# Loading q for two chunks at a time in an attention + MLP kernel, with later stores, halved stripes and two moved chunks

## The chip, the cores and the metric

The kernel runs on one core of one Trainium2 chip. The metric is device time of one execution in microseconds (us); the kernel before takes 227 us. A run is called slow when it lies over 1.5% above the fastest of its kernel. Ratios use fast runs; the medians quoted are of all runs of a kernel, slow ones included.

Engines are named as in the profile: PE is the matrix engine, PEld its weight load, DVE the vector engine, ACT the scalar engine, POOL GpSimd, SP the engine that only issues DMAs here ("SPq" is its queue). A DMA is cut into packets that run on up to 16 DMA engines.

## The reference, cut to what matters

```python
# q, k, v: [4 batches, 8 heads, 768 tokens, 64];  lam: one decay per head
# linear attention with decay, in blocks of tokens, with a running state per head
for b in range(nb):
    intra = (q_b @ k_b.T * Dmask) @ v_b
    inter = (q_b * lam_pow) @ kv_state
    out[b] = intra + inter
    kv_state = lam_block * kv_state + (k_b * rev_pow).T @ v_b
x = out, tokens by (head, dim)           # [3072, 512]
h = x @ w_in                             # [3072, 2048]
g = where(h >= 1, h, where(h <= -1, 0, (h + 1)**2 / 4))
return g @ w_out                         # [3072, 512] float32
```

## The kernel before

There are 24 chunks of 128 tokens (six to a batch) and six stripes of four chunks. For each chunk q, k and v are loaded, q and k are scaled and cast to bf16 on POOL (k of the first four on DVE), transposed (on PE for the first six chunks, by DMA after that), and PE makes the attention output `po`, which ACT casts into `xT`. For each stripe PE makes `h` (512 tokens by 16 blocks of 128), ACT and DVE the activation, and PE the output rows, which ACT copies to an output buffer `osb` and SP stores. The MLP of a stripe is interleaved with the attention of the next ones.

All instructions are emitted in an order that a small planner in the kernel computes beforehand; every engine then works through its own queue in order. SP's queue holds loads, DMA transposes and stores together. An SP entry whose data are not ready holds up everything behind it.

```python
def f_load(c, x, wait):                       # one chunk, one of q, k, v: 256-byte runs
    t = ld.tile([128, H, D], F32, ...)
    nc.sync.dma_start(out=t, in_=(q, k, v)[x][b, :, s0:s0 + C, :].rearrange("h p d -> p h d"))
def f_qx(c):                                  # transpose by DMA, chunks 6 to 23
    nc.sync.dma_start_transpose(out=qT[c], in_=qs[c].rearrange("p h d -> p (h d)"))
def f_x(c):
    nc.scalar.copy(out=xT[sx][:, :, off:off + C], in_=pot[c])
def f_st(s, ms):                              # store: 128 rows of 2 KB
    nc.sync.dma_start(out=out[m0:m0 + 128, :], in_=osb[s, ms])
...
QS = (1, 2)          # stripes whose first matmul is done chunk by chunk (128 columns)
op = tile_pool(bufs=3)                        # output buffers
add(("st", y), "SP", 550, ..., due=-1, dma=780)   # a store goes before any load
# (cut: everything else)
```

## Time and profile before

| What | Value | From |
|---|---|---|
| time, median of 4 runs | 227.14 us | runs |
| span, granted clock | 225.5 us, 0.996 | profile |
| PE busy | 205.6 us | engine table |
| first matmul | 7.5 us | timeline |
| 256-byte, 2 KB packet, median | 18 ns, 85 ns | DMA packet records |
| store, issue to landing | 2.6 us | DMA issues |

These are the lines of the page for the kernel before: busy tenths of PE in 40 slices of the span (5.6 us each), granted clock in tenths, and busy share of the DMA engines.

```profile
PE   0497989999999989689999999999999999999992
PEclk9999999999999999999999999999999999999998
DMA  6999999999898797999999999999011001110212
```

PE is full except for the fill (the first four slices), a dip around slices 14 to 17 (79 to 101 us), and the tail. DMA is busy until 157 us.

The waits of PE in the kernel before, from 60 us on (who waited for whom, total us, times, longest):

```profile
PE pu L266 <- ACT vi L235: 2.3, 2, 1.7
PE ph L332 <- ACT xT L312: 1.0, 1, 1.0
PE py L365 <- issue: 0.2, 1, 0.2
```

So about 3.3 us of PE time are lost after 60 us. Before that there is the fill, and PE's first matmul waits 7.5 us for the first k. `vi` is the cast of v, which waits for v's load. The SP queue before, in that stretch (start us, us, what):

```profile
80.93 0.58 SPq L406 DMA_DIRECT2D x2f<-in_v_dram  x1
82.03 0.36 SPq L374 DMA_DIRECT2D out_dram<-osb  x1
82.45 2.07 SPq L406 DMA_DIRECT2D x1f<-in_k_dram  x1
84.63 1.21 SPq L256 DMA_TRANSPOSE kT<-ks  x1
85.95 1.19 SPq L260 DMA_TRANSPOSE qT<-qs  x1
87.19 0.57 SPq L406 DMA_DIRECT2D x0f<-in_q_dram  x1
87.82 0.57 SPq L406 DMA_DIRECT2D x2f<-in_v_dram  x1
```

SP has hardly a pause: as soon as one entry is issued the next is (the longest pause here is 0.5 us, before the store). Loads, transposes and stores take turns.

### The profile page before, as it was taken

The page shows a single profiled execution, that of the slowest core. Times are in us where ns is not written, and L with a number is a line of the kernel's source. Part 1 is how long each engine was busy: PE and PEld are TensorE (multiplying, and loading weights), DVE is VectorE, ACT ScalarE, POOL GpSimd, SP SyncE. Part 2 cuts the span into 40 slices and gives each one's busy share as a digit, 9 for nine tenths or more (in the row PEclk, how much of TensorE's full clock was granted, in tenths as well). Part 3 has the DMA queues.
Part 4 walks back from the last instruction along what each step waited for, and adds up shares of the span by engine and source line. Part 5 has one row for each costly group of instructions (what it writes and reads, how often), then busy time and mean ns, then how long its engine had stood idle before and what let it go on. Part 6 is the DMA issues. An engine that isn't in the chain of part 4 may idle for free.

```text
span 225.5 us, 4385 instructions
## 1 busy us (share of the span) xinstructions
PE 205.6 (91%) x1733; PEld 123.4 (55%) x1760; DVE 144.2 (64%) x218; ACT 123.6 (55%) x220; POOL 61.0 (27%) x65
## 2 busy tenths in 40 slices
PE   0497989999999989689999999999999999999992
PEld 0376634765888577567664554545545544444441
DVE  7687399978498948567655956856656564554300
ACT  3346867544678285546757575676655444455121
POOL 6543560056034332423342542361000000000000
PEclk9999999999999999999999999999999999999998
DMA  6999999999898797999999999999011001110212
GB/s 121 216 218 170 195 189 202 200 223 196 212 202 158 182 215 169 205 173 204 225 196 237 214 166 233 232 211 211 0 49 47 24 22 49 47 47 16 77 67 77
DMA packets 102837, 34.38 MB, mean 152 GB/s; under 512 B 95136, under 2 KB 99744, under 8 KB 102816
## 3 DMA queue, kind: packets, MB, share of 16 engines
q1 hardware_dynamic: 97920, 29.90, 70.4%
q0 software_dynamic: 4752, 4.19, 12.2%
q8 instruction: 14, 0.23, 0.5%
q14 instruction: 7, 0.06, 0.1%
q10 hardware_dynamic: 144, 0.00, 0.0%
HBM read 27.27 MB, written 6.29 MB: 149 GB/s over the span
## 4 chain that ended last, share of the span: by engine, by line
PE 57%; SPq 3%; DMA 2%; issue 1%; ACT 1%; ACTq 0%
PE py L365 27%; PE ph L332 23%; PE po L305 3%; DMA x2f<-in_v_dram 2%; PE ps L285 2%; SPq L406 1%; PE po L302 1%; PE pu L266 1%; SPq L256 1%; SPq L260 1%; ACT vi L235 0%; ACT osb L370 0%; PE pt L285 0%; ACTq L370 0%
## 5 line engine op out<-in xcount | busy, mean ns | idle before, releaser
L332 PE MATMUL ph<-xT,w_in_sb 128*128 128x128 bf16 (+1 forms) x741 | 92.5, 268 | 1.9 <-ACT xT L312 1.0
L365 PE MATMUL py<-w_out_sb,gT 128*128 128x512 bf16 x368 | 92.6, 379 | 1.0 <-issue 0.2
L340 ACT ACTIVATE r<-ph,one 128x512 bf16<-128x512 f32 (+2 forms) x96 | 64.6, 678 | 47.7 <-PE ph L332 38.4
L332 PEld LDWEIGHTS <-w_in_sb 128*128 128x128 bf16 x752 | 52.5, 98 | 29.0 <-issue 2.2
L365 PEld LDWEIGHTS <-gT 128*128 128x128 bf16 x384 | 35.7, 98 | 38.8 <-DVE gT L356 0.2
L348 DVE TENSOR_SCALAR t<-r 128x1024 bf16<-128x1024 bf16 x48 | 25.2, 526 | 42.7 <-ACT r L340 42.7
L356 DVE TENSOR_TENSOR gT<-w,t 128x1024 bf16<-128x1024 bf16 x48 | 39.8, 828 | 1.6
L231 POOL TENSOR_TENSOR ks<-x1f,tab_k 128x512 bf16<-128x512 f32 x20 | 22.1, 1103 | 62.0 <-DMA x1f<-in_k_dram 48.9
L351 DVE TENSOR_TENSOR w<-r,t 128x1024 bf16<-128x1024 bf16 x48 | 37.2, 775 | 1.5
L231 POOL TENSOR_TENSOR qs<-x0f,tab_q 128x512 bf16<-128x512 f32 x24 | 28.5, 1189 | 25.7 <-DMA x0f<-in_q_dram 25.3
L235 ACT CAST vi<-x2f 128x512 bf16<-128x512 f32 x24 | 14.8, 616 | 16.5 <-DMA x2f<-in_v_dram 16.4
L295 DVE TENSOR_TENSOR sc<-ps,causal 128x512 bf16<-128x512 f32 x20 | 13.8, 689 | 13.6 <-PE pt L285 13.6
L370 ACT COPY osb<-py 128x512 f32<-128x512 f32 x24 | 14.1, 586 | 15.1 <-PE py L365 13.4
L305 PE MATMUL po<-sc,vi 128*128 128x128 bf16 x192 | 19.2, 226 | 0.2
L312 ACT CAST xT<-po 128x512 bf16<-128x512 f32 x24 | 14.0, 585 | 7.2 <-PE po L305 6.6
L270 ACT CAST ubd<-pu 64x256 bf16<-64x256 f32 x40 | 14.6, 364 | 5.3 <-PE pu L266 5.0
L305 PEld LDWEIGHTS <-vi 128*128 128x128 bf16 x192 | 15.2, 102 | 2.3 <-issue 0.6
L302 PE MATMUL po<-qT,ubd 128*128 128x128 bf16 x80 | 15.1, 224 | 0.0
L295 DVE TENSOR_TENSOR sc<-pt,causal 128x512 bf16<-128x512 f32 x20 | 13.6, 680 | 0.0
L266 PE MATMUL pu<-vi,ks 128*128 128x128 bf16 x80 | 8.4, 232 | 2.4 <-ACT vi L235 2.3
L241 PE MATMUL pt<-ident,ks 128*128 128x128 bf16 x24 | 3.1, 266 | 8.0 <-DVE ks L231 7.8
L266 PEld LDWEIGHTS <-ks 128*128 128x128 bf16 x80 | 6.4, 105 | 5.5 <-issue 3.1
(48 smaller groups left out, 87.4 us busy)
## 6 DMA issues: line engine op xcount, KB each, us to landing
x1f<-in_k_dram SPq DMA_DIRECT2D x24, 256.0 KB, 4.8
x0f<-in_q_dram SPq DMA_DIRECT2D x24, 256.0 KB, 4.4
x2f<-in_v_dram SPq DMA_DIRECT2D x24, 256.0 KB, 4.6
out_dram<-osb SPq DMA_DIRECT2D x24, 256.0 KB, 2.6
w_out_sb<-in_moe_w_out_dram POOLq DMA_DIRECT2D x4, 512.0 KB, 13.3
w_in_sb<-in_moe_w_in_dram POOLq DMA_DIRECT2D x3, 512.0 KB, 6.6
w_in_sb<-in_moe_w_in_dram POOLq DMA_DIRECT2D x2, 256.0 KB, 5.0
kT<-ks SPq DMA_TRANSPOSE x18, 4.2
```

Source lines behind the costliest of these rows:

```text
L231: eng.tensor_tensor(t, qkv_ld[c, x], _bc(tab[:, c % NCB, :], 2, D), op=AX.mult)
L235: nc.scalar.copy(out=v_out(vi[c % NV]), in_=qkv_ld[c, 2].rearrange("p (a b) d -> p a b d", b=2))
L266: nc.tensor.matmul(pu[0][:, hp, :], lhsT=pair(ks[c], hp), rhs=v_pair(vi[c % NV], hp), start=(c % NCB == 0 and hp == 0), stop=True, skip_gr ...
L295: nc.vector.tensor_tensor(sc_sb[c][:, g], pst[c, g], _bc(causal, 1, HP), op=AX.mult)
L302: nc.tensor.matmul(po[:, hp], lhsT=ubd[(c - 1) % NUB][:, hp, :], rhs=qT[c][:, hp, :], start=True, stop=False)
L305: nc.tensor.matmul(po[:, hp], lhsT=vi[c % NV][:, hp, hi].rearrange("p a d -> p (a d)"), rhs=sc_sb[c][:, hi, hp, :], start=(cb == 0 and hi ...
L332: nc.tensor.matmul(ph[:, j * m:(j + 1) * m], lhsT=w_in_sb[:, ko, (ni + j) * 128:(ni + j + 1) * 128], rhs=xT[s][:, ko, part * m:(part + 1) ...
L340: nc.scalar.activation(out=r_t[grp][:, i, cs], in_=ph_t[s, ni, part][:, cs], func=AF.Relu, bias=one[:, 0:1])
L348: nc.vector.tensor_scalar(t_t[grp], r, 0.5, 1.0, op0=AX.mult, op1=AX.min)
L351: nc.vector.tensor_tensor(w_t[grp], r, t_t[grp], op=AX.subtract)
L356: nc.vector.tensor_tensor(gT[s][:, f - RW * n:f, part * m:(part + 1) * m], w_t[grp].rearrange("p a (b m) -> p (a b) m", m=m), t_t[grp].rea ...
L365: nc.tensor.matmul(py_t[s, ms], lhsT=gT[s][:, ko, ms * 128:(ms + 1) * 128], rhs=w_out_sb[:, ko, :], start=(ko == 0), stop=(ko == FO - 1))
```

## The change

Its intent: q with 512-byte runs, because they move more bytes in the same DMA time; fewer SP issues; stores out of the way of loads in the stretch where loads are late. In a pair of chunks partition j holds tokens 2j and 2j+1. A chunk's scores therefore come out with even tokens first, then odd ones; the causal mask is permuted to match, and so are the rows of the store.

```diff
-    for x in (1, 0, 2): one load per chunk each for k, q, v
+    # q: one load for two chunks (512 KB), when the chunk is even
+    t = lq.tile([128, H, 2, D], F32, ...)
+    i = q[b, :, s0:s0 + 2 * C, :].rearrange("h (j e) d -> j h (e d)", e=2)
+    nc.sync.dma_start(out=t.rearrange("p h e d -> p h (e d)"), in_=i)
...
+    def q_cols(c, hp, rows=slice(0, 128)):      # columns of chunk c: 64 even, 64 odd tokens
+        x = qT[c // 2][rows, 0, hp, i * 64:(i + 1) * 64]
+        return bass.AP(x.tensor, x.offset, [list(x.ap)[0], [HP * 128, 2], [1, 64]])
...
-        nc.sync.dma_start(out=out[m0:m0 + 128, :], in_=osb[s, ms])
+        nc.sync.dma_start(out=out[m0:m0 + 128, :].rearrange("(j e) n -> e j n", e=2), in_=osb[s, ms])
...
-    op: bufs=3;  ("st", y): due=-1
+    op: bufs=8;  ("st", y): due=0.055            # after the first 46 of 60 loads
...
-    QS = (1, 2)
+    PARTS = {1: 4, 2: 4, 3: 2, 4: 2}             # stripes 3, 4 in halves
-    ORDER = [(0, 0), (0, 1), (0, 2), 4, (0, 3), (0, 4), (1, 0), (1, 1), (1, 2), (1, 3)]
+    ORDER = [(0, 0), (0, 1), (0, 2), (0, 3), 4, (0, 4), (1, 0), (1, 1), 5, (1, 2), (1, 3)]
# (cut: the new tables for q, the planner's entries for pairs)
```

In ORDER `(0, i)` is a block of w_in, `(1, i)` of w_out, and a number is a chunk.

More of the change, by code (lines that the diff above doesn't have):

```diff
@@ L56 @@
     LD = 6
+    LQ, NQ2 = 3, 3
+    NO = 8
+    XQ = 3
     RW, NR = 2, 3
@@ L66 @@
     ld = ctx.enter_context(tc.tile_pool(name="ld", bufs=LD))
+    lq = ctx.enter_context(tc.tile_pool(name="lq", bufs=LQ))
+    qtq = ctx.enter_context(tc.tile_pool(name="qtq", bufs=NQ2))
     qkp = ctx.enter_context(tc.tile_pool(name="qkp", bufs=NQK))
@@ L72 @@
     rp = ctx.enter_context(tc.tile_pool(name="rp", bufs=NR))
-    op = ctx.enter_context(tc.tile_pool(name="op", bufs=3))
+    op = ctx.enter_context(tc.tile_pool(name="op", bufs=NO))
     PS = bass.MemoryType.PSUM
@@ L97 @@
     nc.scalar.activation(out=ln_lam, in_=lam_b, func=AF.Ln)
-    pos_i = const.tile([128, NCB], I32)
-    nc.gpsimd.iota(pos_i, pattern=[[C, NCB]], base=-S // 2, channel_multiplier=1)
+    pos_i = const.tile([128, 2, NCB], I32)
+    nc.gpsimd.iota(pos_i[:, 0], pattern=[[C, NCB]], base=-S // 2, channel_multiplier=1)
+    nc.gpsimd.iota(pos_i[:, 1], pattern=[[1, 2], [2 * C, NCB // 2]], base=-S // 2, channel_multiplier=2)
     causal = const.tile([128, 128], F32)
@@ L103 @@
         out=causal, in_=causal, compare_op=AX.is_ge, fill=0.0,
-        base=0, pattern=[[1, 128]], channel_multiplier=-1)
+        base=0, pattern=[[1, 2], [2, 64]], channel_multiplier=-1)
     NKB, NUB, NV = 3, 3, 4
@@ L112 @@
     nc.vector.memset(kbd[0], 0.0)
-    pos = const.tile([128, NCB], F32)
+    pos = const.tile([128, 2, NCB], F32)
     nc.vector.tensor_copy(pos, pos_i)
@@ L118 @@
         nc.gpsimd.memset(t, 0.0)
-    arg = const.tile([128, NCB, H], F32)
-    nc.vector.tensor_tensor(arg, _bc(pos, 2, H), _bc(ln_lam, 1, NCB), op=AX.mult)
-    tab_q = const.tile([128, NCB, H], F32)
-    nc.scalar.activation(out=tab_q, in_=arg, func=AF.Exp)
+    arg = const.tile([128, 2, NCB, H], F32)
+    nc.vector.tensor_tensor(arg.rearrange("p a c h -> p (a c) h"), _bc(pos.rearrange("p a c -> p (a c)"), 2, H),
+                            _bc(ln_lam, 1, 2 * NCB), op=AX.mult)
     tab_k = const.tile([128, NCB, H], F32)
-    nc.scalar.activation(out=tab_k, in_=arg, func=AF.Exp, scale=-1.0)
+    nc.scalar.activation(out=tab_k, in_=arg[:, 0], func=AF.Exp, scale=-1.0)
+    tab_q = const.tile([128, 2, NCB // 2, H], F32)
+    nc.scalar.activation(out=tab_q.rearrange("p a c h -> p (a c) h"), in_=arg[:, 1], func=AF.Exp)
     for t in ubd + kbd[1:]:
@@ L226, in pair, with cast @@
         return t[:, 2 * hp:2 * hp + 2, :].rearrange("p a d -> p (a d)")
-    def cast(c, x, eng):
-        tab, d, nm = ((tab_q, qs, "qs"), (tab_k, ks, "ks"))[x]
-        t = qkp.tile([128, H, D], BF16, name=nm, tag=nm)
-        eng.tensor_tensor(t, qkv_ld[c, x], _bc(tab[:, c % NCB, :], 2, D), op=AX.mult)
-        d[c] = t
+    def cast(c, eng):
+        ks[c] = qkp.tile([128, H, D], BF16, name="ks", tag="ks")
+        eng.tensor_tensor(ks[c], qkv_ld[c, 1], _bc(tab_k[:, c % NCB, :], 2, D), op=AX.mult)
@@ new lines, in cast_q, with qT_tile @@
+    def cast_q(m, e, eng):
+        qs[m, e] = qkp.tile([128, H, D], BF16, name="qs", tag="qs")
+        eng.tensor_tensor(qs[m, e], qkv_ld[m, 0][:, :, e], _bc(tab_q[:, e, m % (NCB // 2), :], 2, D), op=AX.mult)
+    def qT_tile(m):
+        if m not in qT:
+            qT[m] = qtq.tile([128, 2, HP, 128], BF16, name="qT", tag="qT")
+        return qT[m]
+    def q_cols(c, hp, rows=slice(0, 128)):
+        i = c % 2
+        x = qT[c // 2][rows, 0, hp, i * 64:(i + 1) * 64]
+        return bass.AP(x.tensor, x.offset, [list(x.ap)[0], [HP * 128, 2], [1, 64]])
@@ L234, in cast_v, with f_t @@
     def cast_v(c):
         nc.scalar.copy(out=v_out(vi[c % NV]), in_=qkv_ld[c, 2].rearrange("p (a b) d -> p a b d", b=2))
-    def f_t(c, i):
-        if i:
-            ptt[c] = pp_t.tile([128, 2, HP, 128], BF16, name="pt", tag="pt")
+    def f_t(c):
+        ptt[c] = pp_t.tile([128, HP, 128], BF16, name="pt", tag="pt")
         for hp in range(HP):
-            nc.tensor.transpose(out=ptt[c][:, i, hp, :], in_=pair((qs, ks)[i][c], hp), identity=ident)
+            nc.tensor.transpose(out=ptt[c][:, hp, :], in_=pair(ks[c], hp), identity=ident)
@@ L243, in f_kb, with f_tq @@
+    def f_tq(m, e):
+        if ("q", m) not in ptt:
+            pl, nm = (pp_y, "py") if 2 * m < CPS else (pp_t, "pt")
+            ptt["q", m] = pl.tile([128, 2, HP, 128], BF16, name=nm, tag=nm)
+        for hp in range(HP):
+            nc.tensor.transpose(out=ptt["q", m][:, e, hp, :], in_=pair(qs[m, e], hp), identity=ident)
     def f_kb(c, hi):
-        nc.vector.tensor_copy(kbd[c % NKB][HD[hi], :, hi, :], ptt[c][HD[hi], 1])
-    def f_qT(c, e):
-        qT[c] = qtp.tile([128, HP, 128], BF16, name="qT", tag="qT")
-        (nc.scalar.copy if e == "ACT" else nc.vector.tensor_copy)(qT[c], ptt[c][:, 0])
+        nc.vector.tensor_copy(kbd[c % NKB][HD[hi], :, hi, :], ptt[c][HD[hi]])
@@ L250, in f_kT, with f_qT @@
+    def f_qT(m, e):
+        nc.scalar.copy(qT_tile(m)[:, e], ptt["q", m][:, e])
     def f_kT(c):
         kT[c] = qtp.tile([128, HP, 128], BF16, name="kT", tag="kT")
-        nc.vector.tensor_copy(kT[c], ptt[c][:, 1])
+        nc.vector.tensor_copy(kT[c], ptt[c])
     def f_kx(c):
@@ L256, in f_kx, with f_qx @@
         nc.sync.dma_start_transpose(out=kT[c], in_=ks[c].rearrange("p h d -> p (h d)"))
-    def f_qx(c):
-        qT[c] = qtp.tile([128, HP, 128], BF16, name="qT", tag="qT")
-        nc.sync.dma_start_transpose(out=qT[c], in_=qs[c].rearrange("p h d -> p (h d)"))
+    def f_qx(m, e):
+        nc.sync.dma_start_transpose(out=qT_tile(m)[:, e], in_=qs[m, e].rearrange("p h d -> p (h d)"))
     def f_u(c):
@@ L272, in f_s @@
     def f_s(c, g):
-        pl, nm = (pp_s, "ps") if g == 0 else ((pp_h, "ph"), (pp_h, "ph"), (pp_y, "py"), (pp_t, "pt"))[c]
+        pl, nm = (pp_s, "ps") if g == 0 else ((pp_h, "ph"), (pp_h, "ph"), (pp_t, "pt"), (pp_t, "pt"))[c]
         pst[c, g] = pl.tile([128, HP, 128], F32, name=nm, tag=nm)
@@ L277, in f_s @@
                 nc.tensor.matmul(pst[c, g][:, 2 * hi + j, :], lhsT=kbd[c % NKB][:, 2 * g + j, hi, :],
-                                 rhs=qT[c][:, 2 * g + j, :], start=True, stop=True)
+                                 rhs=q_cols(c, 2 * g + j), start=True, stop=True)
     def f_s2(c):
@@ L284, in f_s2 @@
             for hi in range(2):
-                nc.tensor.matmul(pst[c, hi][:, hp, :], lhsT=kT[c][HD[hi], hp, :], rhs=qT[c][HD[hi], hp, :],
+                nc.tensor.matmul(pst[c, hi][:, hp, :], lhsT=kT[c][HD[hi], hp, :], rhs=q_cols(c, hp, HD[hi]),
                                  start=True, stop=True)
@@ L301, in f_o @@
             if cb > 0:
-                nc.tensor.matmul(po[:, hp], lhsT=ubd[(c - 1) % NUB][:, hp, :], rhs=qT[c][:, hp, :],
+                nc.tensor.matmul(po[:, hp], lhsT=ubd[(c - 1) % NUB][:, hp, :], rhs=q_cols(c, hp),
                                  start=True, stop=False)
@@ L373, in f_st @@
         m0 = s * MS + ms * 128
-        nc.sync.dma_start(out=out[m0:m0 + 128, :], in_=osb[s, ms])
+        nc.sync.dma_start(out=out[m0:m0 + 128, :].rearrange("(j e) n -> e j n", e=2), in_=osb[s, ms])
     T0, STEP, LEAD = 22000, 1057, 3000
-    QS = (1, 2)
+    PARTS = {1: 4, 2: 4, 3: 2, 4: 2}
     l_seq = [(1, 0, i, 0) for i in range(FO)]
     for s in range(1, NST + 1):
-        if s in QS:
-            l1 = [(1, s, i, p) for p in range(CPS) for i in range(0, FO, CPS)]
-        else:
-            l1 = [(1, s, i, 0) for i in range(FO)]
+        n = PARTS.get(s, 1)
+        l1 = [(1, s, i, p) for p in range(n) for i in range(0, FO, n)]
         l2 = [(ms, kg) for ms in range(CPS) for kg in range(CPS)]
@@ L398, in o_due @@
             return T0 - LEAD - (CPS - 1 - i) * 3550
-        if s in QS:
-            return l_due[1, s, 0, i] - LEAD
+        if s in PARTS:
+            n = PARTS[s]
+            return l_due[1, s, 0, i * n // CPS] - LEAD - (CPS // n - 1 - i % (CPS // n)) * 3000
         return first[s] - LEAD - (CPS - 1 - i) * (first[s] - first[s - 1]) / CPS
     def f_load(c, x, wait):
-        t = ld.tile([128, H, D], F32, name=f"x{x}f", tag=f"x{x}f")
         b, s0 = c // NCB, (c % NCB) * C
-        d = nc.sync.dma_start(out=t, in_=(q, k, v)[x][b, :, s0:s0 + C, :].rearrange("h p d -> p h d"))
+        if x == 0:
+            t = lq.tile([128, H, 2, D], F32, name="x0f", tag="x0f")
+            i = q[b, :, s0:s0 + 2 * C, :].rearrange("h (j e) d -> j h (e d)", e=2)
+            d = nc.sync.dma_start(out=t.rearrange("p h e d -> p h (e d)"), in_=i)
+            qkv_ld[c // 2, 0] = t
+        else:
+            t = ld.tile([128, H, D], F32, name=f"x{x}f", tag=f"x{x}f")
+            d = nc.sync.dma_start(out=t, in_=(k, v)[x - 1][b, :, s0:s0 + C, :].rearrange("h p d -> p h d"))
+            qkv_ld[c, x] = t
         if wait is not None:
             tc.add_manual_dep(d.ins, w_dma[wait].ins.name, SYNC)
-        qkv_ld[c, x] = t
     def f_w(it, wait):
@@ L424 @@
             add(("w",) + it, "POOL", 900, lambda it=it, wait=gated: f_w(it, wait),
-                [("w",) + w_seen[-1], ("cast", CPS - 1, 0) if len(w_seen) > 1 else None] if w_seen else [("cast", CPS - 2, 0), ("cast", CPS - 2, 1)], due=pos_ * 1e-3, dma=3100 if it[0] else 775 * W_IN[it[1]])
+                [("w",) + w_seen[-1], ("cast", CPS - 1, 1) if len(w_seen) > 1 else None] if w_seen else [("cast", CPS - 2, 2), ("cast", CPS - 2, 1)], due=pos_ * 1e-3, dma=3130 if it[0] else {2: 1900, 4: 3130}[W_IN[it[1]]])
             OPS[("w",) + it].gate = gated is not None
@@ L430 @@
         gated = len(w_seen) - 2 if last_c is not None and w_seen and not isinstance(order[order.index(it) - 1], int) else None
-        for x in (1, 0, 2):
-            add(("ld", it, x), "SP", 590, lambda i=it, x=x, wait=gated if x == 1 else None: f_load(i, x, wait),
-                [("cast", it - LD, x), ("w",) + w_seen[-2] if w_seen else None], due=pos_ * 1e-3, dma=1190)
+        for x in (1, 2) if it % 2 else (1, 0, 2) if it == 0 else (0, 1, 2):
+            need = [("w",) + w_seen[-2] if w_seen else None]
+            if x == 0:
+                add(("lq", it // 2), "SP", 700, lambda i=it: f_load(i, 0, None),
+                    [("cq", it // 2 - LQ, 0), ("cq", it // 2 - LQ, 1)] + need, due=pos_ * 1e-3, dma=1800)
+            else:
+                add(("ld", it, x), "SP", 590, lambda i=it, x=x, wait=gated if x == 1 else None: f_load(i, x, wait),
+                    [("cast", it - LD, x)] + need, due=pos_ * 1e-3, dma=1190)
             pos_ += 1
@@ L439 @@
         lastu = c - 1 if cb else c - 2
-        for x in (1, 0):
-            e = "DVE" if c < CPS and x else "POOL"
-            add(("cast", c, x), e, 690 if e == "DVE" else 1060,
-                lambda c=c, x=x, eng=(nc.vector if e == "DVE" else nc.gpsimd): cast(c, x, eng),
-                [("ld", c, x), ("cast", c - 1, x), ("t", c - NQK), ("tq", c - NQK), ("u", c - NQK) if x else ("qT", c - NQK)])
+        m = c // 2
+        e = "DVE" if c < CPS else "POOL"
+        add(("cast", c, 1), e, 690 if e == "DVE" else 1060, lambda c=c, eng=(nc.vector if e == "DVE" else nc.gpsimd): cast(c, eng),
+            [("ld", c, 1), ("cast", c - 1, 1), ("t", c - NQK), ("u", c - NQK)])
@@ L445 @@
         add(("cast", c, 2), "ACT", 640, lambda c=c: cast_v(c),
             [("ld", c, 2), ("o", c - NV), ("u", c - NV), ("cast", c - 1, 2)])
-        if c < XT:
-            for x, prev in ((1, [("kT", c - 1), ("kb", c - 1, 0), ("kb", c - 1, 1), ("qT", c - 1), ("m", c - 1, 1) if c >= CPS else None]), (0, [("t", c)])):
-                add(("t", c) if x else ("tq", c), "PE", mm(*[128] * 4), lambda c=c, x=x: f_t(c, x), [("cast", c, x)] + prev,
-                    due=od - 6000, extra=FILL)
-            e = "ACT" if c < CPS else "DVE"
-            add(("qT", c), e, 600 if c < CPS else 365, lambda c=c, e=e: f_qT(c, e), [("tq", c), ("o", c - NQT), ("qT", c - 1)])
-        else:
-            add(("t", c), "SP", 1200, lambda c=c: f_kx(c), [("cast", c, 1), ("m", c - NQT, 1)], due=-2, dma=860)
-            add(("qT", c), "SP", 1200, lambda c=c: f_qx(c), [("cast", c, 0), ("o", c - NQT)], due=-2, dma=860)
+        for i in range(2 if c % 2 == 0 else 0):
+            old = ("tq", m - NQK // 2, i)
+            add(("cq", m, i), "POOL", 1060, lambda m=m, i=i: cast_q(m, i, nc.gpsimd),
+                [("lq", m), ("cq", m, 0) if i else None, old, ("qT",) + old[1:]])
+            if m < XQ:
+                add(("tq", m, i), "PE", mm(*[128] * 4), lambda m=m, i=i: f_tq(m, i),
+                    [("cq", m, i)] + ([("kT", c - 1), ("m", c - 1, 1), ("tq", m, 0) if i else None] if c >= CPS else []),
+                    due=od - 6000, extra=FILL)
+                add(("qT", m, i), "ACT", 600, lambda m=m, i=i: f_qT(m, i), [("tq", m, i)])
+            else:
+                add(("qT", m, i), "SP", 1200, lambda m=m, i=i: f_qx(m, i), [("cq", m, i), ("o", 2 * (m - NQ2) + 1)], due=-2, dma=640)
@@ new lines @@
+        if c < XT:
+            add(("t", c), "PE", mm(*[128] * 4), lambda c=c: f_t(c),
+                [("cast", c, 1), ("kT", c - 1), ("kb", c - 1, 0), ("kb", c - 1, 1), ("m", c - 1, 1) if c > 2 else None,
+                 ("qT", m, 0) if c >= CPS and c % 2 == 0 and m < XQ else None, ("qT", m, 1) if c >= CPS and c % 2 == 0 and m < XQ else None],
+                due=od - 6000, extra=FILL)
+        else:
+            add(("t", c), "SP", 1200, lambda c=c: f_kx(c), [("cast", c, 1), ("m", c - NQT, 1)], due=-2, dma=640)
@@ L466 @@
             add(("s", c, 0), "PE", mm(*[128] * 4) + 190, lambda c=c: f_s2(c),
-                [("kT", c) if c < XT else ("t", c), ("qT", c), ("m", c - 1, 0), ("m", c - 1, 1)], due=od - 2500, extra=FILL)
+                [("kT", c) if c < XT else ("t", c), ("qT", m, 0), ("qT", m, 1), ("m", c - 1, 0), ("m", c - 1, 1)], due=od - 2500, extra=FILL)
         for h in range(2):
@@ L470 @@
                 add(("s", c, h), "PE", mm(*[128] * 4), lambda c=c, h=h: f_s(c, h),
-                    [("kb", c, 0), ("kb", c, 1), ("qT", c), ("m", c - 1, 0) if not h else None], due=od - 3000 + 100 * h, extra=FILL)
+                    [("kb", c, 0), ("kb", c, 1), ("qT", m, 0), ("qT", m, 1), ("m", c - 1, 0) if not h else ("t", c)], due=od - 3000 + 100 * h, extra=FILL)
             add(("m", c, h), "DVE", 690, lambda c=c, h=h: f_m(c, h), [("s", c, h if c < CPS else 0), ("o", c - 3), ("m", c, 0) if h else None])
@@ L487 @@
     for n1, (_, s, i, p) in enumerate(l1_order):
-        n = CPS if s in QS else 1
-        kx = [("x", s * CPS + p)] if n > 1 else [("x", s * CPS + CPS - 1)]
+        n = PARTS.get(s, 1)
+        kx = [("x", s * CPS + (p + 1) * CPS // n - 1)]
         rw = RW
@@ L504 @@
     for n2, (_, s, ms, kg) in enumerate(l2_order):
-        if s in QS:
-            need = [("g", (s * FO + 4 * ms + 3) // RW)]
+        n = PARTS.get(s, 1)
+        if n > 1:
+            need = [("g", (s * FO + (ms * n // CPS + 1) * FO // n - 1) // RW)]
         else:
@@ L512 @@
         if kg == 3:
-            add(("y", y), "ACT", 600, lambda a=(s, ms): f_y(*a), [("l2", n2), ("y", y - 1), ("st", y - 3)])
-            add(("st", y), "SP", 550, lambda a=(s, ms): f_st(*a), [("y", y), ("st", y - 1)], due=-1, dma=780)
+            add(("y", y), "ACT", 600, lambda a=(s, ms): f_y(*a), [("l2", n2), ("y", y - 1), ("st", y - NO)])
+            add(("st", y), "SP", 550, lambda a=(s, ms): f_st(*a), [("y", y), ("st", y - 1)], due=0.055, dma=780)
     run_plan({"PE": 7000, "ACT": 6500, "DVE": 6000, "POOL": 7000, "SP": 800})
```

## The prediction

> **What bounds it now.** The span is 225.5 us, granted clock 0.996. By the records of single matmuls (512 columns every 0.216 us, 128 every 0.056 us) PE has about 190 us of work. Lost, by stage (busy time by windows, matmul starts): about 17 us before 30 us (fill: first matmul at 7.5 us, then four chunks wait for loads and a chain of casts, transposes and copies, 4 us apart); about 4 us between 78 and 99 us; 0.6 to 1.0 us per 10 us elsewhere (instruction overhead); 3.9 us after the last matmul. From 100 us to 221 us PE is 99% busy.
>
> The 78-99 us gaps (1.0, 1.7, 0.7 us) are, in the chain of waits, v loads and xT that come late. The SP queue is why: from 42 to 156 us it issues without a pause (load 0.57 to 1.1 us, transpose 1.2 us), and stores wait in it for osb ahead of loads. It also waited 17.8 us for w_out before chunk 5. DMA time is the second reason: 256-byte packets take 18 ns, so a 256 KB load is 64 packets per engine, 1.15 us; 2 KB packets take 85 ns.
>
> **What the change does.**
> - q in 512-byte runs: estimate from 18 and 85 ns: 27 ns, 1.75 us a pair instead of 2.3. The Trainium skill (DMA: Bandwidth & Descriptors, "Specifications") gives 512 bytes as the least for line rate; the trace's 14 GB/s an engine at 256 bytes against 24 at 2 KB agrees in direction. 12 issues (about 8 us of SP) and 6 us of DMA go, half of it before 100 us.
> - Late stores, eight buffers: SP no longer holds loads behind osb: 2 to 3 of the 4 us at 78-99.
> - Chunk 5 before the last w_out blocks, chunk 4 after w_in: loads are ahead sooner.
> - Fill: chunk 0 now needs two q casts (1.04 us each) and two copies (0.58) before its scores, about 1.5 us later; chunks 1 and 3 need none; loads are done 1.2 us sooner. Net gain 0 to 1.5 us.
> - Halves in stripes 3, 4: 128 more matmuls, about 3 ns each side: 0.5 to 0.8 us lost, since PE waits for nothing there.
>
> Sum: about -3.5 us.
>
> **The risk.** The store's DRAM side becomes [2, 64, 512]. The same page ("Why a DMA increments its semaphore by 16 and not by 1", on how many engines) says the engine count divides the outermost sizes of both sides: 2 here. No run so far shows it; today's stores are 128 packets on 16 engines (8 x 85 ns each). On two engines one store is 64 x 85 = 5.4 us, 24 are 130 us on rings that loads share: loads would starve and the last four stores alone would add 10 us; 250 to 280 us in all. I give it three in ten: a change tuned with measured DMA costs that still books a store at 0.78 us speaks against it.
>
> **Time.** 223.0 us, range 217 to 230. Faster by over 2%: 0.36; within 2%: 0.36; slower: 0.28.
>
> **What would show it.** Right: q packets of 512 bytes near 27 ns; no PE gap over 1 us between 75 and 100 us; last loads before 150 us; stores landing in 2 to 3 us. Fill: xT of chunk 3 at 24 us or before. Wrong by the risk: median store landing above 5 us, a tail after the last matmul of over 8 us, x2f or x1f leading PE's waits after 100 us. Also wrong if two q casts on POOL make the fill grow.

## The result

The changed kernel takes 283.9 us (median of 4 runs, 282.59 to 286.11), and is correct. The ratio to the kernel before is 1.252, 95% interval 1.243 to 1.261. A ratio here is the mean time of one kernel's fast runs over that of the other's fast runs of the same rounds, so it is not quite the ratio of the medians quoted. The forecast of 217 to 230 us is missed by far. What came is the risk that the prediction had put at three in ten.

The same three lines of the page after (slices of 7.0 us; the end of the PE line is the tail after the last matmul):

```profile
PE   0869899999899989939000009997999999999700
PEclk9999999999999999997755556999999999999965
DMA  6999999969999999919211299967931111111110
```

Two blocks of zeros are new for PE: a hole near the middle, and the end. The clock falls with the first. DMA is not the busy party in the hole: the mean of 16 engines reads 1 or 2 tenths. The three largest waits of PE after, over the whole span (the second is the fill):

```profile
PE ph L356 <- ACT xT L336: 35.6, 3, 34.5
PE pt L260 <- DVE ks L237: 8.3, 2, 7.7
PE pu L290 <- ACT ubd L294: 4.3, 1, 4.3
```

One wait is 34.5 us long. The SP queue after, in and before the hole:

```profile
113.10 1.21 SPq L281 DMA_TRANSPOSE kT<-ks  x1
114.36 0.69 SPq L398 DMA_DIRECT2D out_dram<-osb  x1
115.10 0.42 SPq L435 DMA_DIRECT2D x1f<-in_k_dram  x1
115.58 8.05 SPq L398 DMA_DIRECT2D out_dram<-osb  x2
123.75 7.88 SPq L284 DMA_TRANSPOSE qT<-qs  x2
131.68 21.41 SPq L398 DMA_DIRECT2D out_dram<-osb  x6
153.14 4.95 SPq L435 DMA_DIRECT2D x2f<-in_v_dram  x1
158.21 6.08 SPq L281 DMA_TRANSPOSE kT<-ks  x1
```

The buffered stores come due from 114 us on. From 115 us issuing itself gets slow: six stores take 21.4 us of SP's time, where the kernel before issued one in 0.36 us (median). The v load that PE needs stands behind them until 153 us. At the end the last ACT copy into `osb` ends at 266.6 us, and the span at 281.9: a tail of 15.3 us, against 3.3 us before (222.2 to 225.5).

The DMA packet records say why. The duration of a 2 KB packet is as before (84 ns against 85). What differs is how many are under way at once: before, most often 16 (8.0 of the 28 us in which there are any); after, never more than 4, and exactly 2 for 125 of the 136 us in which there are any. A store has 128 packets. On two engines that is 64 x 84 ns = 5.4 us instead of 8 x 85 ns = 0.68 us. Each load's share for those two engines would then stand behind the stores. The packet records do not name the engine, so this last step is read, not seen; it fits that the v load issued from 153.1 us on is cast only at 167.4 us, where a v load before landed 4.6 us after its issue (median). All 24 stores together have 283 us of packet time, so 141 us on each of two engines.

The sum: 34.5 us of hole, 4.3 us of an earlier wait and 12 us of tail are 51 of the 56 us that the span grew. The earlier wait is the stores' doing as well: ACT stood 6.7 us, until 123.7 us, for a store to free one of the eight output buffers, and the casts that PE needed stood behind it in ACT's queue. Most of the rest is half clock. By the trace's clock records it is 0.50 from 126.5 to 129.9 us, and until 174.3 us, where matmuls had resumed at 169.0. That is 8.7 us of work at half speed, by estimate 4.3 us lost.

### The profile page after: what moved, and what is told of

Its sections match the earlier page's. It is cut to its first block, busy times and chain, and to the rows that moved or that the text cites. A ratio compares the mean times of both kernels' runs of the same rounds, so it can differ in the third digit from the quotient of the medians.

```text
span 281.9 us, 4652 instructions
## 1 busy us (share of the span) xinstructions
PE 210.2 (75%) x1888; PEld 136.8 (49%) x1888; DVE 144.8 (51%) x216; ACT 122.9 (44%) x222; POOL 62.3 (22%) x66
## 4 chain that ended last, share of the span: by engine, by line
PE 37%; DMA 26%; SPq 23%; issue 4%; POOL 3%; ACT 1%; POOLq 0%
PE py L389 20%; PE ph L356 14%; SPq L398 8%; SPq L435 7%; DMA x2f<-in_v_dram 7%; DMA w_out_sb<-in_moe_w_out_dram 6%; SPq L284 4%; DMA x0f<-in_q_dram 4%; DMA x1f<-in_k_dram 4%; DMA w_in_sb<-in_moe_w_in_dram 4%; SPq L281 3%; PE po L329 1%; DMA kT<-ks 1%; POOL qs L241 1%; POOL ks L237 1%
## 5 line engine op out<-in xcount | busy, mean ns | idle before, releaser
L356 PE MATMUL ph<-xT,w_in_sb 128*128 128x128 bf16 (+2 forms) x880 | 95.5, 258 | 37.8 <-ACT xT L336 35.6
L389 PE MATMUL py<-w_out_sb,gT 128*128 128x512 bf16 x384 | 96.7, 384 | 0.1
L356 PEld LDWEIGHTS <-w_in_sb 128*128 128x128 bf16 x880 | 66.1, 99 | 62.7 <-issue 40.3
L372 DVE TENSOR_SCALAR t<-r 128x1024 bf16<-128x1024 bf16 x48 | 27.0, 562 | 79.6 <-ACT r L364 79.5
L237 POOL TENSOR_TENSOR ks<-x1f,tab_k 128x512 bf16<-128x512 f32 x20 | 24.1, 1204 | 69.4 <-DMA x1f<-in_k_dram 65.3
L241 POOL TENSOR_TENSOR qs<-x0f,tab_q 128x512 bf16<-128x512 f32 x24 | 27.6, 1168 | 49.9 <-DMA x0f<-in_q_dram 36.2
L375 DVE TENSOR_TENSOR w<-r,t 128x1024 bf16<-128x1024 bf16 x48 | 37.8, 788 | 1.4
L309 PE MATMUL ps<-qT,kT 64*128 64x128 bf16 x80 | 8.1, 223 | 1.9 <-DMA kT<-ks 1.9
```

Source lines behind the costliest of these rows:

```text
L237: eng.tensor_tensor(ks[c], qkv_ld[c, 1], _bc(tab_k[:, c % NCB, :], 2, D), op=AX.mult)
L241: eng.tensor_tensor(qs[m, e], qkv_ld[m, 0][:, :, e], _bc(tab_q[:, e, m % (NCB // 2), :], 2, D), op=AX.mult)
L356: nc.tensor.matmul(ph[:, j * m:(j + 1) * m], lhsT=w_in_sb[:, ko, (ni + j) * 128:(ni + j + 1) * 128], rhs=xT[s][:, ko, part * m:(part + 1) ...
L372: nc.vector.tensor_scalar(t_t[grp], r, 0.5, 1.0, op0=AX.mult, op1=AX.min)
L375: nc.vector.tensor_tensor(w_t[grp], r, t_t[grp], op=AX.subtract)
L389: nc.tensor.matmul(py_t[s, ms], lhsT=gT[s][:, ko, ms * 128:(ms + 1) * 128], rhs=w_out_sb[:, ko, :], start=(ko == 0), stop=(ko == FO - 1))
```

## The experiments

Eighteen kernels were run, in five calls. Each call timed the kernel before on the same chip, too; its medians there are 226.7, 227.3, 227.0, 227.2 and 227.4 us. "Ratio" is to those.

### 1. Is it the store, and only its engine count?

**The one line, alone, on the kernel before** (`b_e2`; wrong result, since rows come out permuted):

```diff
-        nc.sync.dma_start(out=out[m0:m0 + 128, :], in_=osb[s, ms])
+        nc.sync.dma_start(out=out[m0:m0 + 128, :].rearrange("(j e) n -> e j n", e=2), in_=osb[s, ms])
```

> The kernel before with one line changed: the store writes the DRAM rows as [2, 64, 512]. The result is wrong on purpose (rows permuted within blocks of 128). Theory: 24 stores at 64 x 85 ns = 5.4 us each on two engines, tail after the last matmul 10 us longer or more, loads wait behind stores: 250 to 290 us. Rival: within 2% of before.

283.2 us, ratio 1.247 (1.241 to 1.254). One line gives the kernel before the time of the whole change. At most 4 packets of 2 KB are under way at once there, too. That the two times agree so closely is in part chance: the stores are early here, PE's waits are many (21.6 us in eight waits for a transposed q, the longest after the fill 6.7 us, for `xT`), and the rest of the change costs some us by itself, as the cures show.

**The same with 16 as outermost size** (`b_e16`; also wrong), `e=16` in that line:

> The kernel before with the store's DRAM rows as [16, 8, 512]; wrong result on purpose, rows permuted within blocks of 128. Theory (only the outermost size counts): 16 engines again, 8 packets each, within 1% of before. Rival (the scattered row order in DRAM, or the third dimension of the access pattern, makes the store slow): as slow as the [2, 64, 512] run.

230.2 us, ratio 1.014 (1.009 to 1.019). A scattered order of rows and a third dimension are therefore not what costs 25%; the outermost size is. But the expectation of "within 1%" was missed by a little: 2 KB packets take 123 ns on average there, against 95, and stores land in 3.2 us instead of 2.6. Why was not looked into. (`a_split`, next, writes rows that lie two apart and has slow packets as well, 138 ns on average.)

**Three cures in the changed kernel.** Two stores of 64 rows each, so that 64 is outermost on both sides (`a_split`):

```diff
-        nc.sync.dma_start(out=out[m0:m0 + 128, :].rearrange("(j e) n -> e j n", e=2), in_=osb[s, ms])
+        o = out[m0:m0 + 128, :].rearrange("(j e) n -> e j n", e=2)
+        for e in range(2):
+            nc.sync.dma_start(out=o[e], in_=osb[s, ms][e * 64:(e + 1) * 64, :])
```

> Theory (store on two DMA engines): each store is cut into two of 64 partitions, each with 64 as outermost size on both sides, so all 16 engines carry it again. Everything else of the change stays. Time 219 to 226 us, 2 KB packets up to 16 at once, tail after the last matmul about 4 us. Rival (the loss comes from the late stores' place in the SP order, or from the q pairs, or the halves): still above 260 us with a hole in PE between 134 and 169 us.

235.5 us, ratio 1.037. The store was the 48 us, but the cured change is still slower than before, not faster: the expectation is missed. Token order restored where PE reads q, so that the store is that of before (`a_nat`):

```diff
-        return bass.AP(x.tensor, x.offset, [list(x.ap)[0], [HP * 128, 2], [1, 64]])
+        return bass.AP(x.tensor, x.offset, [list(x.ap)[0], [1, 64], [HP * 128, 2]])
```

(with the causal mask and the store of before.)

> The change with another cure: the scores and outputs read q columns in token order (even and odd tokens interleaved, a step of 1 KB between neighbours), so the store needs no permuted rows and is that of before. Theory: stores on 16 engines, 219 to 226 us. If interleaved reads slow the matmul, its 128-column matmuls with qT take longer than 56 ns apart, 32 x 128 columns a chunk pair, and it is slower than the run with two stores per block; if not, it is the same or 1 us faster for 24 fewer SP issues of 0.5 us.

233.9 us, ratio 1.032. Reading q with a step of 1 KB between neighbours costs PE: matmuls with qT start 0.125 us apart instead of 0.056. Per chunk there are eight such starts for scores and state, so about 0.55 us, by estimate 11 us over 20 chunks; PE shows no gap above 1.2 us after the fill, and is slow instead. Its expectation had said that slow reads would make it slower than `a_split`; it is not, and it is only 3.6 us slower than the next cure. That one has a gap of 2.0 us and half clock after it (section 2); `a_nat` has neither. Here are two of those lines of `a_nat` in the timeline of PE, with a pair of score matmuls at each start:

```profile
139.90 0.28 PE L309 MATMUL ps<-qT,kT 64*128 64x128 bf16 x1
140.02 0.28 PE L309 MATMUL ps<-qT,kT 64*128 64x128 bf16 x1
```

The Trainium skill (SBUF — State Buffer, "Door 1: The DMA port swizzle") says that accesses that leave a 16-byte line pay a penalty; the 0.125 us here fit that in direction. The third cure puts the tokens back where nobody pays, in the ACT copy from PSUM to `xT` (`a_fx`):

```diff
-        nc.scalar.copy(out=xT[sx][:, :, off:off + C], in_=pot[c])
+        nc.scalar.copy(out=xT[sx][:, :, off:off + C].rearrange("p h (j e) -> p h j e", e=2),
+                       in_=pot[c].rearrange("p h (e j) -> p h j e", e=2))
```

> The change, with token order restored in the copy of po to xT (ScalarE writes even and odd tokens back to their places), so the store is one DMA of 128 rows on 16 engines as before, and PE reads q in runs of 64. The stores stay late, with eight buffers. Theory (after the two-engine store is cured, the burst of late stores in the SP queue is what costs: in the run with two stores per block 18 stores were issued between 113 and 129 us ahead of a v load, PE then stood 5.8 us and its clock fell to half): half as many issues, so a shorter hole of 1 to 4 us near 115 to 130 us, 226 to 232 us. Rival (something else in the change costs, such as the q pairs or halves): hole gone but the time still above 230 us. If the permuting copy costs ScalarE, xT casts go above 0.59 us.

230.3 us, ratio 1.017 (1.011 to 1.022). The copy takes 585 ns as before (median). This is the best form of the whole change, and within its expectation of 226 to 232 us.

### 2. What is still wrong in the cured change? First suspect: the burst of late stores

In `a_split` the SP queue showed this:

```profile
115.40 3.50 SPq L400 DMA_DIRECT2D out_dram<-osb  x4
119.01 2.58 SPq L284 DMA_TRANSPOSE qT<-qs  x2
121.64 7.62 SPq L400 DMA_DIRECT2D out_dram<-osb  x12
129.31 0.60 SPq L437 DMA_DIRECT2D x2f<-in_v_dram  x1
```

PE then stands for 5.8 us (`134.28`, waiting for `xT`). The windows of `a_split` around it (start:end, length, busy us of PE, PEld, DVE, ACT, POOL with counts, granted clock, DMA share, GB/s):

```profile
128.00:132.00 4.00, 0.48 (x3) 0.10 (x1) 0.00 (x0) 0.00 (x0) 0.00 (x0) 0.88 0.90 206
132.00:134.00 2.00, 0.00 (x0) 0.00 (x0) 0.00 (x0) 1.36 (x3) 0.00 (x0) 0.50 0.82 181
134.00:136.00 2.00, 1.72 (x9) 1.19 (x9) 1.11 (x2) 0.82 (x2) 0.88 (x1) 0.50 1.13 247
136.00:138.00 2.00, 1.78 (x7) 0.80 (x7) 1.42 (x2) 1.21 (x2) 0.18 (x1) 0.54 1.19 282
```

The clock drops to 0.50 in the hole and stays there until almost 138 us, so a hole costs more than its length. The Trainium skill (TensorE: Matmul & The Clock Gate, "What's actually happening") describes this half clock after an idle window of about 3.4 us. This trace agrees on the half clock, but not on the time: by its clock records the clock fell at 131.0 us, 2.5 us after PE's last matmul had ended (128.5 us).

The theory is that late stores bunch and block a load, and that early stores are better. The edit for `a_fx_early` and `a_split_early`, on top of the cures:

```diff
-    NO = 8                                   # and ("st", y): due=0.055
+    NO = 3                                   # and ("st", y): due=-1
```

> As the run before it, but stores with the priority they had before (first) and three output buffers. Theory: no burst, no PE gap above 2 us after 100 us; the fill gains 1.5 us, 222 to 226 us, at or below the kernel before. Rival: late stores were a help, so without them loads wait behind stores from 50 to 100 us and it is slower than the run with late stores.

> Two stores per block on 16 engines with stores first and three buffers. Theory: 24 more SP issues spread out cost less than the burst: 225 to 230 us, so 5 to 10 us below the run with two stores per block and late stores. Rival (24 more issues themselves are the cost, in an SP queue with no slack from 50 to 140 us): stays above 233 us.

Both went the wrong way: `a_fx_early` 233.4 us, ratio 1.025; `a_split_early` 239.4 us, ratio 1.056. Late stores help the changed kernel, by 2.2 us with `a_fx` (mean of fast runs, 230.4 against 232.6), in spite of the burst. That early stores are better is refuted. That the burst costs nothing is not: `a_fx` still has one PE gap, 2.0 us at 128.1 us, and it follows a burst. Its SP queue:

```profile
120.92 3.33 SPq L399 DMA_DIRECT2D out_dram<-osb  x6
124.31 0.63 SPq L436 DMA_DIRECT2D x2f<-in_v_dram  x1
```

The v load behind the six stores is cast at 128.48 us, `xT` at 129.48, and PE goes on at 130.12, with half clock from 131.1 to 134.5 us. The gap and, by estimate, 1.7 us of half clock are 3.7 of the 4.5 us by which the profiled `a_fx` is longer than the profiled `b_late8`, which comes next. `a_fx_early` has no such gap, but waits of 6.6 us for the activation.

Late stores alone, on the kernel before (`b_late8`):

> The kernel before with late stores and eight buffers alone, all else as before, stores on 16 engines. Theory: the burst of up to 8 stores (0.4 to 0.6 us of SP each, 0.7 us of DMA each) costs 1 to 6 us in stage 3, less what loads gain before 100 us (up to 3.8 us): 225 to 231 us. The prediction's step said it would be worth 2 to 3 us: 224 us.

225.2 us, ratio 0.994 (0.988 to 1.000): a small gain if any. In the profile, PE's waits for v and xT between 60 and 100 us are gone; the one large wait that is left is 1.4 us near 145 us. So it does what the prediction had said, though worth 1 to 2 us, not 2 to 3.

### 3. Taking the rest apart

Four kernels, each set against `b_late8` or `a_fx`. Halves undone in the cured change (`a_fx_whole`: `PARTS = {1: 4, 2: 4}`), then the chunk order undone as well, which leaves q pairs and late stores alone (`a_fx_whole_order`); and halves alone (`b_late8_half`) and the chunk order alone (`b_late8_order`) on top of late stores in the kernel before.

> The change with token order restored in the copy of po to xT and one store of 16 engines, late stores, but stripes 3 and 4 whole as before. Theory (halves let the plan ask for the second half's chunks just in time, so the burst of stores catches them): the hole at 128 us and the slow clock after it go, 225 to 227 us. Rival (q pairs cost: one late pair holds two chunks): still 229 us or more.

> As the run before it, with chunk 4 and 5 also back at their old place: only the q pairs and late stores are left of the change. Set against late stores alone (225.2 us in the earlier call) it gives what q pairs are worth. The prediction said 2 to 3 us faster by fewer SP issues and less DMA time: 222 to 224 us. Rival (pairs cost more than they save): 226 us or more.

> The kernel before with late stores and eight buffers, and stripes 3 and 4 in halves; no q pairs. Theory (halves cost by just-in-time chunks): 228 to 231 us with a hole near the start of a half. The prediction's step: halves cost 0.5 to 0.8 us, so 226 us.

> The kernel before with late stores and eight buffers, and chunk 4 after the fourth w_in block, chunk 5 between w_out blocks. Theory: chunk 5 early takes load off 42 to 60 us; 224 to 225.5 us. Rival (w_out later delays the second matmul of stage 0): 226 us or more.

| Kernel | q pairs | halves | order | us | ratio | 95% |
|---|---|---|---|---|---|---|
| `b_late8` | no | no | no | 225.2 | 0.994 | 0.988 to 1.000 |
| `b_late8_half` | no | yes | no | 226.6 | 0.993 | 0.984 to 1.002 |
| `b_late8_order` | no | no | yes | 225.6 | 0.990 | 0.983 to 0.998 |
| `a_fx_whole_order` | yes | no | no | 234.0 | 1.027 | 1.017 to 1.036 |
| `a_fx_whole` | yes | no | yes | 231.5 | 1.016 | 1.009 to 1.024 |
| `a_fx` | yes | yes | yes | 230.3 | 1.017 | 1.011 to 1.022 |

All have late stores. `b_late8` and `a_fx` ran in one call, the other four in another. In that other call two of the seven runs of the kernel before took 229.4 and 229.7 us and count as fast; without them the four ratios would be 0.997, 0.994, 1.031 and 1.020, in the order of the table.

Halves do not change the time by anything that these runs can tell, and alone they make no hole: that expectation is refuted. The chunk order is worth 1% with pairs (234.0 against 231.5 us); without pairs nothing is shown. q pairs cost 3%: 1.027 over 0.994 is 1.033, or 7.4 us. With the chunk order in both, they cost 2.6% (231.5 against 225.6 us). They had been expected to gain. "q pairs" stands here for all that comes with them: the loads, the second table of factors, the permuted reads and copy, the planner's entries. One more thing differs: `due=0.055` lets stores in after 46 of 72 loads in `b_late8` (first store at 96 us), but after 46 of 60 with pairs (116 us in `a_fx_whole_order`). PE's gaps of 2.1 and 1.4 us at 82 and 95 us come before any store; the one of 2.5 us at 152 us comes after, and what the place of the stores has to do with it was not tested.

### 4. Why do q pairs cost?

They do save DMA time: from 60 to 80 us the DMA share is 0.88 with pairs (`a_fx_whole_order`, at 175 GB/s) and 1.31 without (`b_late8`, at 190 GB/s). (The share is the summed time of packets over that of 16 engines, and passes 1 where packets of an engine overlap.) By these traces they lose in the round trip, at least with stripes 3 and 4 whole: PE is busy for 35.8 of the 40 us from 60 to 100 us in `a_fx_whole_order`, 39.4 in `b_late8`. With halves and moved chunks (`a_fx`) it is 39.0; there the burst of section 2 is most of what is left. SP queue of the pairs kernel, one pair:

```profile
89.78 0.57 SPq L432 DMA_DIRECT2D x0f<-in_q_dram  x1
90.45 1.21 SPq L281 DMA_TRANSPOSE kT<-ks  x1
91.72 0.57 SPq L436 DMA_DIRECT2D x1f<-in_k_dram  x1
92.38 0.96 SPq L436 DMA_DIRECT2D x2f<-in_v_dram  x1
93.39 2.30 SPq L436 DMA_DIRECT2D x1f<-in_k_dram  x1
95.78 1.20 SPq L436 DMA_DIRECT2D x2f<-in_v_dram  x1
97.09 2.96 SPq L284 DMA_TRANSPOSE qT<-qs  x2
100.15 1.21 SPq L281 DMA_TRANSPOSE kT<-ks  x1
101.41 0.57 SPq L432 DMA_DIRECT2D x0f<-in_q_dram  x1
```

and POOL's casts of the same pair (with the idle time before and what ended it):

```profile
94.45 2.04 POOL L241 TENSOR_TENSOR qs<-x0f,tab_q 128x512 bf16<-128x512 f32 x2 [5.19 <-DMA x0f<-in_q_dram]
97.56 1.04 POOL L237 TENSOR_TENSOR ks<-x1f,tab_k 128x512 bf16<-128x512 f32 x1 [1.07 <-DMA x1f<-in_k_dram]
99.56 1.04 POOL L237 TENSOR_TENSOR ks<-x1f,tab_k 128x512 bf16<-128x512 f32 x1 [0.95 <-DMA x1f<-in_k_dram]
```

The q load lands 4.7 us after its issue, is cast at once, and the transposes that need that cast stand in the same SP queue, behind four more loads. The next q load stands behind those transposes. The pair kernel runs this loop once in 11.8 us (q casts at 82.24, 94.45, 106.28 and 117.76 us), 5.9 us a chunk. `b_late8` makes a chunk in 5.3 us, somewhat earlier (k casts from 66.28 to 98.18 us, six chunks), with loads and transposes alternating. In the chain of waits of the pairs kernel from 66 to 103 us, PE's h matmuls are only 7%, the rest mostly loads, SP issue, transposes and casts:

```profile
by line: DMA x1f<-in_k_dram 28.7%; DMA x2f<-in_v_dram 15.4%; SPq L436 14.1%; SPq L281 11.7%; PE ph L357 7.0%; DMA kT<-ks 6.7%; POOL ks L237 4.5%; ACT r L365 3.8%; issue 2.9%; ACT vi L255 1.7%; SPq L432 1.5%; PE pu L290 1.0%; PE ps L309 0.9%
```

**First test: plan five transfers in flight instead of three** (`RING = 5`), to get loads ahead of transposes: on q pairs alone, on late stores alone, on the cured change, and on late stores with the chunk order.

> q pairs and late stores alone (no halves, chunk order of before, token order restored in the copy to xT), with the plan allowed five transfers in flight instead of three, so some loads go ahead of the transposes in the SP queue. Theory (unoverlapped round trip): the gaps at 82, 95 and 151 us shrink, 227 to 230 us instead of 234. Rival (the pair itself costs): 233 to 235 us.

> Control: the kernel before with late stores and eight buffers (225.2 us) and five transfers in flight in the plan. Theory: its round trip of 5.3 us a chunk is already under the 8.2 us that PE takes for a chunk, so at most 1 us faster: 224 to 226 us. Rival: five in flight is good or bad for every kernel alike, then it moves by as much as the pair kernel does.

> The whole change with the store cured in the copy to xT, and five transfers in flight. Theory: 230.3 us falls to 225 to 228 us, as the hole at 128 us goes. Rival: stays at 229 to 231 us.

> The fastest kernel so far (late stores, chunks 4 and 5 moved: 225.6 us in its call, ratio 0.990) with five transfers in flight. Theory: 223 to 225.5 us. It is also the candidate for a version that beats both.

237.8 us (1.044), 230.4 us (1.008), 230.5 us (1.012) and 226.6 us (0.996). (These ratios count two runs of the kernel before at 229.2 and 229.4 us; without them they would be 1.049, 1.015, 1.017 and 1.001.) None of the gains came, and the control moved by about as much as the pairs kernel. The new order had also put some v loads behind transposes, so several things changed at once. This test decides nothing, except that five is shown to be better than three in none of the four.

**Second test: the form of the transfer, and the transposes.** `pairs_256` fetches each pair by two loads of 256-byte runs into the same tile, in the same place of every queue:

```diff
-            i = q[b, :, s0:s0 + 2 * C, :].rearrange("h (j e) d -> j h (e d)", e=2)
-            d = nc.sync.dma_start(out=t.rearrange("p h e d -> p h (e d)"), in_=i)
+            i = q[b, :, s0:s0 + 2 * C, :].rearrange("h (j e) d -> e j h d", e=2)
+            for e in range(2):
+                d = nc.sync.dma_start(out=t[:, :, e], in_=i[e])
```

`pairs_pe` makes all q transposes on PE (`XQ = 12` instead of 3), so SP loses 18 entries of 1.2 us, and PE gets 72 matmuls more, 4 us.

> q pairs and late stores alone (234.0 us, ratio 1.027), but each pair of chunks is fetched by two loads of 256-byte runs into the same tile, in the same place of every queue. If the order and the round trip cost, and not the form of the transfer: 1.025 to 1.040 of before, as 12 more issues of 0.6 us and 0.55 us more DMA time a pair come on top. If the big transfer itself costs (it lands late or holds up transposes behind it): below 1.015.

> q pairs and late stores alone, but all q transposes on PE as for the first six chunks, so SP issues 18 transposes of 1.2 us less and the next loads don't stand behind them. PE gets 72 matmuls of 0.056 us more, 4 us, and ScalarE 18 copies of 0.59 us. Theory (the round trip through SP costs): the chunk period between 60 and 110 us falls from 5.9 to 5.3 us or less, PE's waits for kT and xT after 60 us fall from 6 us to under 2 us, and time is 230 to 233 us in spite of the 4 us more work. Rival (not the SP queue): waits stay, 237 us or more.

`pairs_256`: 238.1 us, ratio 1.045 (1.038 to 1.053; its profiled run was a slow one and is not used here). Big transfers are thus not the trouble; the ratio lies even above the 1.025 to 1.040 that was expected for that case. On the contrary, one load of 512-byte runs in place of two of 256-byte runs is worth 1.8% (1.045 over 1.027) once the pairs are there; the 12 SP issues that it saves are part of this.

`pairs_pe`: 227.7 us, ratio 1.002 (0.997 to 1.007). With 4 us more PE work it is 2.4% faster than the same kernel with DMA transposes, and better than expected. The wait list of PE from 60 us on shrinks from these four lines (`a_fx_whole_order`):

```profile
PE ps L309 <- DMA kT<-ks: 3.9, 3, 2.1
PE ph L357 <- ACT xT L336: 2.5, 1, 2.5
PE ph L357 <- ACT r L365: 2.0, 3, 0.9
PE py L390 <- issue: 0.6, 4, 0.2
```

to this one (`pairs_pe`):

```profile
PE ps L309 <- ACT qT L273: 1.3, 1, 1.3
```

and POOL's q casts come at 66.34, 75.32, 84.39, 93.30 and 101.15 us, 4.4 us a chunk instead of 5.9. That the q transposes by DMA limit the pairs kernel is therefore shown by taking them away. Whether they do so by their place in the SP queue, or by their own time (3.3 us from issue to landing in `a_fx_whole_order`, median), this run does not separate; and its first store comes at 98 us instead of 116. That pairs make the same queue worse than single chunks do because loads and transposes come in larger clumps is read from the two traces (5.9 against 5.3 us a chunk); no run isolated it. So why pairs cost what they do stays in part open. Whether the kernel before would gain from PE transposes, too, was not run.

### The fastest version

Late stores with eight buffers, and the moved chunks, on the kernel before with its own q loads (`b_late8_order`): 225.6 us, ratio 0.990 (0.983 to 0.998). It is 20% faster than the change as given. Against the kernel before the gain is 1% at most: 0.6% without the two runs at 229.4 and 229.7 us. Nor is it told apart from `b_late8` (0.994). Its PE waits from 60 us on are short ones, the longest 0.9 us.

## Why the prediction was wrong, point by point

- **The failed step is the weighing of the risk.** The sum of -3.5 us has no term for the store: it keeps each one on 16 engines. The runs showed it on two, and 48 us for that (283.9 against 235.5 us with the store split). The mechanism was named, with the right source and nearly the right size. The Trainium skill (DMA: Bandwidth & Descriptors, "Why a DMA increments its semaphore by 16 and not by 1") lets the engine count divide the outermost sizes of both sides; a store of [2, 64, 512] has 2. The trace gives 2 packets at once, 5.4 us a store (forecast 5.4), and 283.9 us (forecast 250 to 280 for this case). It was given three in ten "because" a change whose author had measured DMA costs would not book a store at 0.78 us. That is a guess about the author, set against a rule on the hardware and an access pattern that stood in the diff. The guess lost. But a better weighing would not have saved the rest of the sum: with the store cured the change is still 1.7% slower (`a_fx`), where the sum said 1.5% faster. The next points show where.
- **"The last four stores alone would add 10 us"**: the tail grew by 12 us. Nearly right. That loads would starve throughout was only partly right: with late stores nothing happened until 114 us, then everything at once.
- **q in 512-byte runs, 27 ns a packet**: measured 27.0 ns (median). DMA time fell as computed. But the step from DMA time and issue count to a gain failed. Measured: 5.9 to 7.4 us lost. SP's queue was full, as the prediction itself said; what counted, as far as the traces tell, was the order and the round trip through cast and transpose, not the number of issues.
- **Late stores, 2 to 3 us**: measured 0.6%, 1.3 us, at the edge of what the runs resolve. Its mechanism (no gap between 78 and 99 us) is seen.
- **Chunks 4 and 5 moved**: no number was given. Nothing shown without pairs (0.990 against 0.994), 1% with them.
- **Fill, gain 0 to 1.5 us**: xT of chunk 3 is cast at 22.8 us instead of 25.3. Right in direction, and more than forecast.
- **Halves, 0.5 to 0.8 us lost**: not measurable (0.993 against 0.994).

## What to carry to other kernels

Before a DMA's access pattern is changed, look at the outermost size on each side: here a permutation of rows that is free in bytes took the transfer from 16 packets at once to 2, and the loads in the same queue went down with it. If a permutation must be undone, do it in a copy between on-chip memories that is there anyway. In an in-order DMA queue that is also waited on for compute, fewer and larger transfers need not be a gain, as here: count the time from one load, through its cast and transpose, to the next load that stands behind them.

## What the Trainium skill lacked or had wrong

- DMA: Bandwidth & Descriptors ("Why a DMA increments its semaphore by 16 and not by 1"): the rule for the engine count is right here, and the page repeats it among its rules for kernel authors, but without a cost. Here it is 5.4 us against 0.68 us of transfer for one 256 KB store, and 25% of a kernel.
- The same page, "Specifications": at least 512 bytes for line rate. Here a 512-byte packet of q takes 27 ns (19 GB/s an engine), a 256-byte one 18 ns (14 GB/s) and a 2 KB one 84 ns (24 GB/s), so 512 bytes are not yet at the rate of 2 KB.
- The same page has nothing on the order of rows within a DMA of 16 engines: [16, 8, 512] in place of [128, 512] raised the mean 2 KB packet from 95 to 123 ns and the kernel's time by 1.4%. Two stores of [64, 512] with rows two apart (`a_split`) have 138 ns.
- SBUF — State Buffer ("Door 1: The DMA port swizzle") has the penalty outside a 16-byte line without a figure for a matmul: a moving operand of 128 bf16 columns whose neighbours are 1 KB apart took 0.125 us instead of 0.056.
- TensorE: Matmul & The Clock Gate ("What's actually happening") gives about 3.4 us of idle before the clock halves. In `a_fx` a stop of 2.0 us (128.1 to 130.1 us) was followed by a granted clock of 0.50 from 131.1 to 134.5 us; in `a_fx_whole_order` a stop of 2.5 us (151.6 to 154.1 us) left it at 1.00. The length of a stop alone does not decide.
- No page that was read deals with round trips through one in-order DMA queue that holds loads and transposes; here that is 5.9 against 5.3 us a chunk, and 2.4% of the kernel when the q transposes leave the queue.
